# Retention plus feed-forward: groups of two units taken from two batches, and weight DMAs issued closer behind each other

## The chip, the cores and the metric

One core of one Trainium2 chip. The metric is the device time of one execution in microseconds (us); lower is better. Every comparison below uses fast executions of both kernels, taken in turn on the same chip; the experiments were run on three chips, and the kernel before took 292.2 to 292.5 us (medians) on each. A ratio is the mean time of one kernel's fast runs over that of the other's in the same rounds, so it is not quite the ratio of the medians that are quoted.

The engines are TensorE (PE in the profile; PEld is its weight load), VectorE (DVE), ScalarE (ACT), GpSimd (POOL) and SyncE (SP, which here only issues DMAs).

## The reference, cut to what matters

```
scores = 1/8 * q @ k^T                          # (8, 8, 576, 64): batch, head, position, dim
ret    = scores * gamma_h ** (i - j) * (i >= j)   # decay per head, causal
x      = (ret @ v), heads side by side            # 4608 tokens x 512
out    = relu(x @ w_in) ** 2 @ w_out              # 512 -> 2048 -> 512
```

The kernel never makes the 576 x 576 matrix. It goes along a batch in units of 128 positions with a running state R (the decayed sum of k^T v), and feeds each group of two units through the feed-forward. A batch has four full units and a tail of 64 positions; two batches share one tail unit.

## The kernel before

Eighteen groups of two units. Before, the two units of a group follow each other in one batch, so the second needs the state that the first leaves.

```
for bp in range(B // 2):
    for b in (2 * bp, 2 * bp + 1):
        units += [("full", b, c) for c in range(4)]
    units.append(("tail", 2 * bp, 4))
```

The first eight units are loaded as *pairs*: one transfer brings 256 positions of one tensor as 128 partitions, two positions to a partition, in pieces of 512 bytes. k and q of such a pair are cast and transposed on TensorE. The order of all loads at the start is fixed.

```
def add_load_pair(name, u):
    ...
        t = nc.sync.dma_start(out=x, in_=(k, q, v)[n][b, :, c * P:(c + 2) * P, :].rearrange("h (p e) d -> p h (e d)", e=2))
FIRST = ["k0", "q0", "v0", "k2", "q2", "v2", "w0", ..., "w7", "k4", "q4", "v4", "k6", "q6", "v6"]
```

The weights come as eight quarters, w0 to w3 of w_in and w4 to w7 of w_out, issued by GpSimd; the transfer casts them to fp16 on the way. Between these issues GpSimd does other work, ordered by a key (the lowest ready task first).

```
    tile_of["w", i] = nc.gpsimd.dma_start(out=dst, in_=src)
issue = add("POOL", -70 + i, 1.0, fn, deps=issues[-1:], lag=1.6 if issues else 0.0)
```

A part of that other work is the causal mask of the first two groups: half of it is copied out of PSUM by ScalarE and masked by GpSimd (`fp`), the rest is masked by VectorE (`fm`).

```
SHARED = (0, 1)
...
    if a and g in SHARED:
        c = add("ACT", -60 + e, 0.66, fc, deps=[t])
        ms.append(add("POOL", -60 + e, 0.75, fp, deps=[c]))
    else:
        ms.append(add("DVE", base + 5 + e, 0.66, fm, deps=[t] + ms))
```

## Time and profile before

| | before |
|---|---|
| time, median of 3 | 291.88 us |
| span of the profiled run | 290.6 us |
| TensorE busy | 281.6 us (97%) |
| first feed-forward matmul | 17.88 us |
| matmuls of the last w_in quarter (w3) begin | 26.77 us |
| 129th feed-forward matmul (the first of the third group) begins | 54.04 us |
| last matmul begins | 286.72 us |

The feed-forward matmuls (`ph` in the profile) always come in the same number and nearly the same order, so the time at which the n-th of them begins is a clock of the kernel's progress: a difference between two kernels at n is what one has lost by then.

### The profile page before, as it was taken

To read this page: it belongs to the slowest core of one execution; us is meant where nothing else is said; L and a number is where in the kernel's file an instruction comes from. 1 tells how busy PE (TensorE), PEld (TensorE's weight loads), DVE (VectorE), ACT (ScalarE), POOL (GpSimd) and SP (SyncE) were. 2 spreads that over 40 slices of the span, in tenths; PEclk is the share of its full clock that TensorE was granted. 3 is DMA by queue.
4 is the path that set the end of the run, shared out by engine and by line. 5 is a ranking of instruction groups with operands and counts; after the bars stand their busy time and mean duration, and the time that the engine had idled before them with its cause. 6 is when DMAs were issued, how large, how long until landed. Compare 5 with 4: busy or idle time off the path is not lost.

```text
span 290.6 us, 10028 instructions
## 1 busy us (share of the span) xinstructions
PE 281.6 (97%) x4316; PEld 233.6 (80%) x4316; DVE 197.9 (68%) x427; ACT 183.0 (63%) x351; POOL 91.4 (31%) x125
## 2 busy tenths in 40 slices
PE   8978999999999999999999999999999999999995
PEld 3557755688888888888888888888888888888884
DVE  3895369949384849675968767867767876565632
ACT  5654466486767575867767566666767676747830
POOL 5782035525433334241604251615051500000000
PEclk9999999999999999999999999999999999999999
DMA  7999999999999999997959999969699820201004
GB/s 200 275 192 181 182 300 280 215 204 193 235 173 220 208 167 235 219 214 182 190 135 210 200 192 213 204 170 187 161 182 212 167 74 2 74 2 73 2 0 147
DMA packets 139421, 49.94 MB, mean 172 GB/s; under 512 B 118128, under 2 KB 135024, under 8 KB 139376
## 3 DMA queue, kind: packets, MB, share of 16 engines
q1 hardware_dynamic: 134848, 44.84, 75.1%
q0 software_dynamic: 4224, 4.19, 9.1%
q8 instruction: 34, 0.56, 0.8%
q10 hardware_dynamic: 304, 0.26, 0.3%
q14 instruction: 11, 0.09, 0.1%
HBM read 36.70 MB, written 9.44 MB: 159 GB/s over the span
## 4 chain that ended last, share of the span: by engine, by line
PE 88%; DVE 6%; DMA 3%; ACT 1%; issue 1%; POOL 0%; DVEq 0%
PE ph L841 41%; PE po L933 34%; PE psO L339 4%; PE po L881 3%; DMA w_in<-in_moe_w_in_dram 3%; DVE rx L459 2%; PE warm L248 2%; PE psS L339 2%; PE psc L339 2%; DVE vx L396 2%; DVE R L500 1%; PE psT L417 1%; DVE xT L552 0%; ACT rl L849 0%; POOL rx L466 0%
## 5 line engine op out<-in xcount | busy, mean ns | idle before, releaser
L841 PE MATMUL ph<-xT,w_in 128*128 128x256 f16 x1152 | 140.1, 273 | 1.1 <-DMA w_in<-in_moe_w_in_dram 1.1
L841 PEld LDWEIGHTS <-w_in 128*128 128x128 f16 x1152 | 110.6, 98 | 16.6 <-DMA w_in<-in_moe_w_in_dram 1.9
L849 ACT ACTIVATE rl<-ph 128x512 f16<-128x512 f32 x144 | 84.9, 590 | 57.2 <-PE ph L841 55.8
L859 ACT ACTIVATE gT<-rl 128x512 f16<-128x512 f16 x104 | 65.6, 631 | 3.0
L933 PEld LDWEIGHTS <-gS 128*128 128x128 f16 x512 | 49.5, 98 | 6.1 <-DVE gS L910 0.2
L933 PE MATMUL po<-wT,gS 128*128 128x256 f16 x384 | 52.1, 273 | 0.0
L910 DVE TENSOR_TENSOR gS<-gT,gS 128x512 f16<-128x512 f16 x64 | 32.6, 515 | 13.4 <-ACT gT L859 12.7
L933 PEld LDWEIGHTS <-gT 128*128 128x128 f16 x384 | 37.3, 98 | 4.4
L910 DVE TENSOR_TENSOR gS<-gT 128x512 f16<-128x512 f16 x64 | 33.5, 524 | 10.7 <-ACT gT L859 10.5
L933 PE MATMUL po<-w_out,gT 128*128 128x256 f16 x256 | 34.7, 273 | 0.0
L363 POOL TENSOR_TENSOR v<-v,vdec_full 128x512 f16<-128x512 f32 x24 | 26.4, 1100 | 21.7 <-DMA v<-in_v_dram 12.2
L351 POOL CAST kq<-k 128x512 f16<-128x512 f32 x28 | 19.5, 696 | 42.3 <-DMA k<-in_k_dram 40.6
L351 POOL CAST kq<-q 128x512 f16<-128x512 f32 x28 | 19.1, 682 | 42.3 <-DMA q<-in_q_dram 42.3
L861 DVE TENSOR_TENSOR gT<-rl 128x512 f16<-128x512 f16 x40 | 19.5, 489 | 17.6 <-ACT rl L849 17.2
L956 DVE TENSOR_TENSOR o<-po,u 128x256 f32<-128x256 f32 x31 | 13.0, 420 | 14.8 <-PE po L933 9.6
L719 DVE TENSOR_TENSOR xT<-psO,gam_full 128x512 f16<-128x512 f32 x28 | 18.1, 684 | 6.8 <-PE psO L339 6.8
L946 ACT COPY u<-po 128x256 f32<-128x256 f32 x32 | 11.8, 368 | 17.2 <-PE po L933 17.0
L658 DVE TENSOR_TENSOR rT<-psc,mask 128x512 f16<-128x512 f32 x28 | 18.3, 682 | 3.9 <-PE psc L339 3.9
L933 PE MATMUL po<-w_out,gS 128*128 128x256 f16 x128 | 16.9, 273 | 0.0
L933 PE MATMUL po<-wT,gT 128*128 128x256 f16 x128 | 16.6, 273 | 0.0
L881 PE MATMUL po<-w_out,gT 128*128 128x512 f16 x64 | 15.8, 380 | 0.0
L956 DVE TENSOR_TENSOR o<-po,p 128x256 f32<-128x256 f32 x17 | 7.2, 423 | 12.5 <-ACT u L946 6.5
(81 smaller groups left out, 239.6 us busy)
## 6 DMA issues: line engine op xcount, KB each, us to landing
out_dram<-o SPq DMA_DIRECT2D x31, 256.0 KB, 3.5
k<-in_k_dram SPq DMA_DIRECT2D x24, 256.0 KB, 4.4
q<-in_q_dram SPq DMA_DIRECT2D x24, 256.0 KB, 5.0
v<-in_v_dram SPq DMA_DIRECT2D x24, 256.0 KB, 4.9
pair<-in_k_dram SPq DMA_DIRECT2D x4, 512.0 KB, 5.9
pair<-in_q_dram SPq DMA_DIRECT2D x4, 512.0 KB, 6.0
pair<-in_v_dram SPq DMA_DIRECT2D x4, 512.0 KB, 7.0
w_in<-in_moe_w_in_dram POOLq DMA_DIRECT2D x4, 512.0 KB, 7.7
```

Of the source, the lines that this page charges most:

```text
L339: nc.tensor.matmul(out_, lhsT=lhsT, rhs=rhs, start=start, stop=True, skip_group_check=True, tile_position=(64 * row, 64 * col))
L351: op(out=out_.rearrange("p (n b a d) -> p n b a d", n=2, b=2, a=2), in_=in_.rearrange("p (n a b) d -> p n b a d", n=2, a=2))
L363: nc.gpsimd.tensor_tensor(out=t, in0=tile_of["v32", u], in1=vdec[kind].rearrange("p (h o) -> p h o", o=1).to_broadcast([P, H, D]), op=ALU. ...
L658: nc.vector.tensor_tensor(out=r, in0=tile_of["psc", g][:, :, cols(s)].rearrange("p a (n i) -> p a n i", i=64), in1=mask.rearrange("p (o r ...
L841: nc.tensor.matmul(tile_of["ph", g, fb][:, j, :], lhsT=w_in16[:, m, fi * P:(fi + 1) * P], rhs=tile_of["x", g][:, m, :], start=(m == 0), st ...
L849: nc.scalar.activation(out=t, in_=tile_of["ph", g, fb], func=ACTF.Relu)
L859: nc.scalar.activation(out=t, in_=rl, func=ACTF.Square)
L861: nc.vector.tensor_tensor(out=t, in0=rl, in1=rl, op=ALU.mult)
L881: nc.tensor.matmul(tile_of["po", u], lhsT=tile_of["g", g][:, fi, s * P:(s + 1) * P], rhs=w_out16[:, fi, :], start=(fi == 0), stop=(fi == N ...
L910: nc.vector.tensor_tensor(out=Sx(k, h), in0=in0(h), in1=in1(h), op=op)
L933: nc.tensor.matmul(tile_of["pb", g, bank], lhsT=left(i), rhs=right[:, i, :], start=(start and i == 0), stop=(i == HF - 1), skip_group_chec ...
L956: nc.vector.tensor_tensor(out=o_tile(u)[:, half * HM:(half + 1) * HM], in0=bank(x), in1=tile_of[name, g], op=ALU.add)
```

## The change

The intent: with units of two batches in a group, neither needs the other's state, so a state update handles both at once (512 columns in one VectorE instruction where there were two of 256), and the first group needs no state at all. All masks go to VectorE, the squares of the first two groups to ScalarE, and GpSimd issues the weights closer together. Since the units of a pair now lie in different batches, each paired load becomes two transfers of 64 partitions. The diff, cut to its core (the renaming of states from units to groups is left out):

```diff
-        for b in (2 * bp, 2 * bp + 1):
-            units += [("full", b, c) for c in range(4)]
-        units.append(("tail", 2 * bp, 4))
+        units += [("full", b, c) for c in range(4) for b in (2 * bp, 2 * bp + 1)]
+        if bp % 2:
+            units += [("tail", b, 4) for b in (2 * bp - 2, 2 * bp)]
...
-    WARM = 28
+    WARM = 34
-    LAG = {"w0": 1.2, "k4": 0.7, "q4": 0.5}
+    LAG = {"k4": 0.7, "q4": 0.5}
-    SHARED = (0, 1)
+    SHARED = ()
...
-            t = nc.sync.dma_start(out=x, in_=(k, q, v)[n][b, :, c * P:(c + 2) * P, :].rearrange("h (p e) d -> p h (e d)", e=2))
-            if (name, u) == ("k", 4):
-                (wait for w6)
+            for s in range(2):
+                b, c = units[u + s][1:]
+                t = nc.sync.dma_start(out=x[64 * s:64 * s + 64],
+                                      in_=(k, q, v)[n][b, :, c * P:(c + 1) * P, :].rearrange("h (p e) d -> p h (e d)", e=2))
+                if (name, u, s) == ("k", 4, 0):
+                    behind(t, tile_of["w", 5])
...
+            if i == 0:
+                for s in range(2):
+                    behind(tile_of["w", i], tile_of["load", "v", 0, s])
-        issue = add("POOL", -70 + i, 1.0, fn, deps=issues[-1:], lag=1.6 if issues else 0.0)
+        issue = add("POOL", -90 + i, 0.9, fn, deps=issues[-1:] or [loaded["v", 0]], lag=1.0 if issues else 0.0)
...
+        def fr1():
+            r = tile_of["tmp", g] = work.tile([P, 2, NP * D], FP32, name="stmp", tag="stmp", bufs=1)
+            nc.vector.tensor_tensor(out=flat(r), in0=tile_of["psS", g][:, 1], in1=flat(tile_of["Rm", g]), op=ALU.add)
...
-            on_act = g >= STRASSEN and fb in (SQ_ACT if g < last_g - 1 else SQ_LATE)
+            on_act = fb in (SQ_ACT if g < last_g - 1 else SQ_LATE)
```

More of the change, by code (lines that the diff above doesn't have):

```diff
@@ L137 @@
         groups.append(list(range(first, first + n)))
-    groups[-1].reverse()
     STRASSEN = 2
@@ L148 @@
     x_pool = ctx.enter_context(tc.tile_pool(name="x", bufs=3))
-    st_pool = ctx.enter_context(tc.tile_pool(name="st", bufs=6))
+    st_pool = ctx.enter_context(tc.tile_pool(name="st", bufs=1))
     g_pool = ctx.enter_context(tc.tile_pool(name="g", bufs=3))
@@ L230 @@
     JOIN = 7
-    LAG = {"w0": 1.2, "k4": 0.7, "q4": 0.5}
+    LAG = {"k4": 0.7, "q4": 0.5}
     LAG_T, LAG_O = 1.5, 5.0
     PAIRED = 8
-    SHARED = (0, 1)
+    SHARED = ()
     FIRST = ["k0", "q0", "v0", "k2", "q2", "v2", "w0", "w1", "w2", "w3", "w4", "w5", "w6", "w7", "k4", "q4", "v4", "k6", "q6", "v6"]
     sched = Schedule(dict(ff=4, prS=1, prO=1, g=3, ld=5, wst=4, kq=7, v16=7, rT=4, x=3, rl=3, o=4, p1=2, u2=2, u4=2,
-                          R=6, Rm=6, kqT=6))
+                          R=4, Rm=2, kqT=6))
     add = sched.add
@@ L275, with behind @@
     wcast = {}
+    def behind(x, y):
+        tc.add_manual_dep(x.ins, y.ins.name, mybir.DependencyInfo(mybir.DependencyClass.Sync, mybir.DependencyReason.DATA),
+                          reason="order of transfers")
     def add_load(u):
@@ L291, in add_load_pair @@
     def add_load_pair(name, u):
-        b, c = units[u][1:]
         n = "kqv".index(name)
@@ L298, in fn @@
             x = tile_of[name + "32", u] = tile_of["stage", u][:, n % 2]
-            t = nc.sync.dma_start(out=x, in_=(k, q, v)[n][b, :, c * P:(c + 2) * P, :].rearrange("h (p e) d -> p h (e d)", e=2))
-            if (name, u) == ("k", 4):
-                tc.add_manual_dep(t.ins, tile_of["w", 6].ins.name,
-                                  mybir.DependencyInfo(mybir.DependencyClass.Sync, mybir.DependencyReason.DATA),
-                                  reason="the weights come first")
+            for s in range(2):
[4 more added lines that the diff above has]
+                    behind(t, tile_of["w", 5])
+                tile_of["load", name, u, s] = t
         loaded[name, u] = loaded[name, u + 1] = dma_task(0, 1.81 if loaded else 2.9, fn, acq=("wst",) if name != "q" else (),
@@ L315, in fn @@
             tile_of["w", i] = nc.gpsimd.dma_start(out=dst, in_=src)
-        issue = add("POOL", -70 + i, 1.0, fn, deps=issues[-1:], lag=1.6 if issues else 0.0)
-        if not issues:
-            gate.setdefault(("vx", 0), []).append(issue)
+            if i == 0:
+                for s in range(2):
+                    behind(tile_of["w", i], tile_of["load", "v", 0, s])
+        issue = add("POOL", -90 + i, 0.9, fn, deps=issues[-1:] or [loaded["v", 0]], lag=1.0 if issues else 0.0)
         issues.append(issue)
@@ L333 @@
     T = {}
+    first_waits = []
     def quad(out_, lhsT, rhs, row, col, start=True):
-        nc.tensor.matmul(out_, lhsT=lhsT, rhs=rhs, start=start, stop=True, skip_group_check=True,
-                         tile_position=(64 * row, 64 * col))
+        t = nc.tensor.matmul(out_, lhsT=lhsT, rhs=rhs, start=start, stop=True, skip_group_check=True,
+                             tile_position=(64 * row, 64 * col))
+        if first_waits:
+            behind(t, first_waits.pop())
     def half(x):
@@ L408, in add_unit_pair @@
         sched.free("wst", xs["v"])
-        for w in gate.get(("vx", u), []):
-            sched.need(w, xs["v"][0])
         T["kqT", u], T["kqT", u + 1] = [], []
@@ L435, in add_unit_pair, with decay, flat @@
         T["kvx", u] = xs["k"] + xs["v"]
+    def decay(out_, in_, n=2):
+        shape = "p (s n d) -> p s n d"
+        nc.vector.tensor_tensor(
+            out=out_.rearrange(shape, s=n, n=NP), in0=in_.rearrange(shape, s=n, n=NP),
+            in1=dec128.rearrange("p (s n o) -> p s n o", s=1, o=1).to_broadcast([P, n, NP, D]), op=ALU.mult)
+    def flat(x):
+        return x.rearrange("p s n -> p (s n)")
     def add_ret_pair(g):
@@ L488, in add_ret_pair @@
         sched.free("kq", [t])
-        chain = []
-        for s in range(2):
-            src = None if s == 0 and not carry else u + s - 1
-            def fr1(s=s, src=src):
-                r = tile_of["tmp", u + s] = work.tile([P, NP * D], FP32, name="stmp", tag="stmp", bufs=1)
-                nc.vector.tensor_tensor(out=r, in0=rT["sum"][s][:, 0:256], in1=tile_of["R", src], op=ALU.add)
-            def fr2(s=s, src=src):
-                r = tile_of["R", u + s] = st_pool.tile([P, NP * D], FP16, name="R", tag="R")
-                x = rT["sum"][s][:, 0:256] if src is None else tile_of["tmp", u + s]
-                nc.vector.tensor_tensor(
-                    out=r.rearrange("p (n d) -> p n d", d=D), in0=x.rearrange("p (n d) -> p n d", d=D),
-                    in1=dec128.rearrange("p (n o) -> p n o", o=1).to_broadcast([P, NP, D]), op=ALU.mult)
-            if src is not None:
-                chain.append(add("DVE", base + 5.5 + s, 0.42, fr1, deps=[t] + chain[-1:] + [T["R", src]]))
-                T["Rread", src].append(chain[-1])
-                sched.free("ff", chain[-1:])
-            chain.append(add("DVE", base + (6.5 if u == 0 else 5.6) + s, 0.5, fr2, deps=[t] + chain[-1:], acq=("R",)))
-            if src is None:
-                sched.free("ff", chain[-1:])
-            T["R", u + s], T["Rread", u + s] = chain[-1], []
@@ new lines, in fr1, with f, fr2 @@
+        def fr1(s):
+            def f():
+                if s == 0:
+                    tile_of["tmp", g] = work.tile([P, 2, NP * D], FP32, name="stmp", tag="stmp", bufs=1)
+                nc.vector.tensor_tensor(out=tile_of["tmp", g][:, s], in0=rT["sum"][s][:, 0:256], in1=tile_of["R", g - 1][:, s],
+                                        op=ALU.add)
+            return f
+        def fr2(s=None):
+            def f():
+                if s != 1:
+                    tile_of["R", g] = st_pool.tile([P, 2, NP * D], FP16, name="R", tag="R", bufs=4)
+                if s is None:
+                    decay(flat(tile_of["R", g]), flat(tile_of["tmp", g]))
+                else:
+                    decay(tile_of["R", g][:, s], rT["sum"][s][:, 0:256], 1)
+            return f
@@ new lines, in add_ret_pair @@
+        if carry:
+            ts = [add("DVE", base + 5.5 + s / 10, 0.42, fr1(s), deps=[t, T["R", g - 1]]) for s in range(2)]
+            sched.need(ts[1], ts[0])
+            for r in ts:
+                sched.free("ff", [r])
+            T["Rread", g - 1] += ts
+            T["R", g] = add("DVE", base + 5.7, 0.6, fr2(), deps=ts, acq=("R",))
+        else:
+            ts = []
+            for s in range(2):
+                ts.append(add("DVE", base + 26.1 + s / 10, 0.42, fr2(s), deps=[t] + ts,
+                              acq=() if s else ("R",)))
+                sched.free("ff", ts[-1:])
+            T["R", g] = ts[-1]
@@ L512, in inter @@
+        T["Rread", g] = []
         def inter(other):
@@ L515, in inter @@
                     s = a ^ other
-                    if s or carry:
-                        x = 2 * n + b
-                        put2(s, 4 * n + 2 * a + b, tile_of["R", u + s - 1][half(a), half(x)], kqT(s)[half(a), NP + x, :], a)
+                    x = 2 * n + b
+                    put2(s, 4 * n + 2 * a + b, tile_of["R", g - 1][half(a), s, half(x)], kqT(s)[half(a), NP + x, :], a)
         def put2(s, h, lhsT, rhs, row):
@@ L540, in add_ret_pair @@
         t = add("PE", base + 23.9, 0.6, fo1, deps=masked + T["kvx", u], acq=("prO",))
-        t = add("PE", base + 24, 0.75, fo2, deps=[t, T["R", u]] + ([T["R", u - 1]] if carry else []))
+        if carry:
+            t = add("PE", base + 24, 0.75, fo2, deps=[t, T["R", g - 1]])
+            T["Rread", g - 1].append(t)
         for s in range(2):
@@ L544, in add_ret_pair @@
             sched.free("kq", [t])
-            if s or carry:
-                T["Rread", u + s - 1].append(t)
         sched.free("kq", [t])
@@ L569, in cols @@
         return slice(256 * s, 256 * (s + 1))
+    place_of = {units[u]: (group_of[u], u - groups[group_of[u]][0]) for u in range(NU)}
     def states(u):
@@ L574, in states @@
         if kind == "tail":
-            return {0: ("R", u - 5), 1: ("R", u - 1)}
-        return {1: ("Rm", u), 0: ("R", u - 1)} if c else {1: ("Rm", u)}
+            return {i: ("R",) + place_of["full", b + i, 3] for i in range(2)}
+        g, s = place_of[units[u]]
+        return {1: ("Rm", g, s), 0: ("R", g - 1, s)} if c else {1: ("Rm", g, s)}
     def emit_scores(g):
@@ L620, in inter @@
                     x = 2 * n + b
-                    put(g, u, c, 4 * n + 2 * a + b, tile_of[st[c]][half(a), half(x)],
+                    put(g, u, c, 4 * n + 2 * a + b, tile_of[st[c][:2]][half(a), st[c][2], half(x)],
                         tile_of["kqT", u][half(a), NP + x, half(c)], a)
@@ L651, in out1_deps @@
     def out1_deps(g):
-        return [T[x] for u in units_of(g) for x in states(u).values()]
+        return [T[x[:2]] for u in units_of(g) for x in states(u).values()]
     def after_scores(g, t, key):
@@ L657, in fm @@
                 r = tile_of["rT", u] = work.tile([P, 2, NP, 64], FP16, name="rT", tag="rT")
-                nc.vector.tensor_tensor(
+                tile_of["masking", g] = nc.vector.tensor_tensor(
                     out=r, in0=tile_of["psc", g][:, :, cols(s)].rearrange("p a (n i) -> p a n i", i=64),
@@ L665, in after_sums @@
     def after_sums(g, t, key, res):
-        chain = []
-        for s, u in enumerate(units_of(g)):
-            if u not in full_of(g):
-                continue
-            c0 = units[u][2] == 0
-            def fr0(s=s, u=u, c0=c0):
-                r = tile_of["Rm", u] = st_pool.tile([P, NP * D], FP16, name="Rm", tag="Rm")
-                x = tile_of["psS", g][:, 0, cols(s)]
-                if c0:
-                    nc.vector.tensor_copy(out=r, in_=x)
-                else:
-                    nc.vector.tensor_tensor(out=r, in0=x, in1=tile_of["R", u - 1], op=ALU.add)
-            def fr1(s=s, u=u):
-                r = tile_of["tmp", u] = work.tile([P, NP * D], FP32, name="stmp", tag="stmp", bufs=1)
-                nc.vector.tensor_tensor(out=r, in0=tile_of["psS", g][:, 1, cols(s)], in1=tile_of["Rm", u], op=ALU.add)
-            def fr2(s=s, u=u):
-                r = tile_of["R", u] = st_pool.tile([P, NP * D], FP16, name="R", tag="R")
-                nc.vector.tensor_tensor(
-                    out=r.rearrange("p (n d) -> p n d", d=D), in0=tile_of["tmp", u].rearrange("p (n d) -> p n d", d=D),
-                    in1=dec128.rearrange("p (n o) -> p n o", o=1).to_broadcast([P, NP, D]), op=ALU.mult)
-            r0 = add("DVE", key + 0.1 + s, 0.42, fr0, deps=[t] + chain[-1:] + ([] if c0 else [T["R", u - 1]]),
-                     acq=("Rm",))
-            if not c0:
-                T["Rread", u - 1].append(r0)
-            r1 = add("DVE", key + 0.2 + s, 0.42, fr1, deps=[r0])
-            r2 = add("DVE", key + 0.3 + s, 0.5, fr2, deps=[r1], acq=("R",))
-            chain += [r0, r1, r2]
-            T["Rm", u], T["R", u], T["Rread", u], T["Rmread", u] = r0, r2, [], r1
@@ L698, in after_sums, with fr0 @@
-        if chain:
-            sched.free(res, [chain[-2]])
+        if not full_of(g):
+            return
+        c0 = units[full_of(g)[0]][2] == 0
+        def fr0():
+            r = tile_of["Rm", g] = st_pool.tile([P, 2, NP * D], FP16, name="Rm", tag="Rm", bufs=2)
+            x = tile_of["psS", g][:, 0]
+            if c0:
+                nc.vector.tensor_copy(out=flat(r), in_=x)
+            else:
+                nc.vector.tensor_tensor(out=flat(r), in0=x, in1=flat(tile_of["R", g - 1]), op=ALU.add)
@@ new lines, in fr1, with fr2 @@
+        def fr1():
+            r = tile_of["tmp", g] = work.tile([P, 2, NP * D], FP32, name="stmp", tag="stmp", bufs=1)
+            nc.vector.tensor_tensor(out=flat(r), in0=tile_of["psS", g][:, 1], in1=flat(tile_of["Rm", g]), op=ALU.add)
+        def fr2():
+            r = tile_of["R", g] = st_pool.tile([P, 2, NP * D], FP16, name="R", tag="R", bufs=4)
+            decay(flat(r), flat(tile_of["tmp", g]))
+        r0 = add("DVE", key + 0.1, 0.69, fr0, deps=[t] + ([] if c0 else [T["R", g - 1]]), acq=("Rm",))
@@ L701, in after_outs @@
+        if not c0:
+            T["Rread", g - 1].append(r0)
+        r1 = add("DVE", key + 0.2, 0.69, fr1, deps=[r0])
+        r2 = add("DVE", key + 0.3, 0.65, fr2, deps=[r1], acq=("R",))
+        T["Rm", g], T["R", g], T["Rread", g], T["Rmread", g] = r0, r2, [], r1
+        sched.free(res, [r1])
     def after_outs(g, t1, t2, key):
@@ L707, in after_outs @@
             sched.free("rT", [t2])
-            for name, ru in states(u).values():
+            for name, rg, at in states(u).values():
                 if name == "R":
-                    T["Rread", ru].append(t2)
-                else:
-                    sched.free("Rm", [t2, T["Rmread", u]])
+                    T["Rread", rg].append(t2)
+                elif at == 0:
+                    sched.free("Rm", [t2, T["Rmread", rg]])
         for u in us:
@@ L762, in f2 @@
                 emit_sums(g + 1, "prS")
+                if not full_of(g + 1):
+                    first_waits.append(tile_of["masking", g + 1])
                 emit_out2(g)
@@ L767, in add_ret @@
             t2 = add("PE", base + 30, 0.2 + QUAD * (24 * n + 16 * len(full_of(g + 1))), f2,
-                     deps=[t1] + T["masked", g] + T["masked", g + 1] + sums_deps(g + 1), acq=("prS",))
+                     deps=[t1] + T["masked", g] + T["masked", g + 1] + sums_deps(g + 1), acq=("prS",) if full_of(g + 1) else ())
             for u in units_of(g + 1):
@@ L1036 @@
             sched.free("kq", [T["kqread", u]])
-    for u in range(NU):
-        if ("Rread", u) in T:
-            sched.free("R", T["Rread", u])
+    for g in range(len(groups)):
+        if ("Rread", g) in T:
+            sched.free("R", T["Rread", g])
     for g in range(len(groups)):
```

## The prediction

> **What bounds the kernel now.** I read the page's first two parts, then the busy time in five stretches that I chose along the chain of waits, then the TensorE, GpSimd and VectorE rows of the first 60 us, and last the groups by shape.
>
> ```profile
> PE 281.6 (97%) x4316; PEld 233.6 (80%) x4316; DVE 197.9 (68%) x427; ACT 183.0 (63%) x351; POOL 91.4 (31%) x125
> ...
> DMA  7999999999999999997959999969699820201004
> ```
>
> TensorE is the bound, and DMA is full over the first half, as long as weights and inputs both have to come in. The stretches tell where time is not yet matmul:
>
> ```profile
> 0.00:17.88 17.88, 14.81 (x229) 8.03 (x229) 12.03 (x47) 10.13 (x22) 11.48 (x29) 1.00 1.03 227
> 17.88:26.77 8.89, 7.73 (x113) 5.89 (x105) 6.85 (x13) 4.60 (x8) 5.80 (x7) 1.00 1.19 184
> 26.77:57.20 30.43, 29.75 (x400) 19.42 (x400) 21.55 (x37) 16.06 (x30) 9.56 (x12) 1.00 1.11 241
> 57.20:287.00 229.80, 229.34 (x3592) 200.25 (x3584) 157.08 (x330) 152.25 (x293) 64.59 (x79) 1.00 0.80 159
> ```
>
> The columns are the stretch, its length, then busy us of PE, PEld, DVE, ACT, POOL, the clock, DMA share and GB/s. From 57.2 us to 287 us TensorE idles 0.46 us of 229.8: nothing done to VectorE there can pay. The first useful feed-forward matmul starts at 17.88 us, and most of the "busy" before it is warm-up on junk. Until 26.77 us the feed-forward waits for w_in:
>
> ```profile
> 17.88 1.92 PE L841 MATMUL ph<-xT,w_in 128*128 128x256 f16 x16
> 20.14 1.05 PE L841 MATMUL ph<-xT,w_in 128*128 128x256 f16 x8 [0.34 <-DMA w_in<-in_moe_w_in_dram]
> ...
> 23.51 2.79 PE L841 MATMUL ph<-xT,w_in 128*128 128x256 f16 x24 [0.26 <-DMA w_in<-in_moe_w_in_dram]
> 26.77 2.79 PE L841 MATMUL ph<-xT,w_in 128*128 128x256 f16 x24 [0.47 <-DMA w_in<-in_moe_w_in_dram]
> ```
>
> Each bracket is a weight quarter landing: w1 at 20.1, w2 at 23.5, w3 at 26.7. After w3 TensorE is full. So the head's bound is the time at which w3 lands, and the end comes later or earlier with it. Why the quarters are 3.3 us apart is seen on GpSimd, which issues them between its own work:
>
> ```profile
> 9.77 0.99 POOL L315 DMA_DIRECT2D w_in<-in_moe_w_in_dram  x1
> ...
> 11.34 2.29 POOL L466 TENSOR_TENSOR rx<-rx,mask 128x512 f16<-128x512 f16 x2
> 13.57 1.00 POOL L315 DMA_DIRECT2D w_in<-in_moe_w_in_dram  x1
> ...
> 15.59 0.80 POOL L315 DMA_DIRECT2D w_in<-in_moe_w_in_dram  x1
> 17.62 1.15 POOL L466 TENSOR_TENSOR rx<-rx,mask 128x512 f16<-128x512 f16 x1 [1.24 <-ACT rx L463]
> 18.73 0.81 POOL L315 DMA_DIRECT2D w_in<-in_moe_w_in_dram  x1
> ```
>
> w3 is issued only at 18.73, behind a masking step, and lands 7.99 us later (a row of the chain of waits). The four w_out parts, issued back to back from 20.67 us, come 2.5 us apart: that is the rate DMA can give.
>
> [...] the same decay multiply takes 0.41 us from PSUM, and 1.39 us from SBUF while GpSimd masks from 11.34 to 13.63:
>
> ```profile
> 11.56 0.41 DVE L500 TENSOR_TENSOR R<-psS,dec 128x256 f16<-128x256 f32 x1
> ...
> 12.54 1.39 DVE L500 TENSOR_TENSOR R<-stmp,dec 128x256 f16<-128x256 f32 x1
> ```
>
> [...] Before, only the tails are loaded as halves, in 256-byte pieces:
>
> ```profile
> 4.50:12.50 8.00, 7.58 (x102) 4.27 (x101) 5.25 (x11) 3.80 (x8) 4.00 (x7) 1.00 1.20 291
> 34.50:36.50 2.00, 2.00 (x17) 1.41 (x16) 0.85 (x2) 0.64 (x2) 0.00 (x0) 1.00 0.55 113
> 48.00:49.50 1.50, 1.50 (x38) 0.84 (x39) 1.50 (x4) 1.48 (x4) 0.61 (x1) 1.00 1.34 217
> 66.00:68.00 2.00, 2.00 (x20) 1.63 (x19) 2.00 (x3) 1.92 (x5) 1.50 (x3) 1.00 1.33 222
> ```
>
> Half tiles (48 us) and whole tiles (66 us) both give about 220 GB/s at 256 bytes, so the trace doesn't decide it. The paired loads (4.5 us) run at 291 with 512-byte pieces on whole tiles. The change cuts just these in halves.
>
> **The change part by part.**
>
> *State updates for both units at once.* Per group 2 x (0.416 + 0.423 + 0.523) = 2.72 us of VectorE become three 512-column instructions. PSUM readers of that shape take 0.68 us (the 128x512 mask rows), so about 0.68 + 0.68 + 0.65 = 2.0 us: 0.7 us less in each of 12 groups, some 8 us of VectorE. TensorE idles 0.46 us in that whole stretch, so on the path: at most 0.2 us. The number of quadrant matmuls is equal: the inter-batch terms left out of groups 0 and 2 (8 each) are now all 16 left out of group 0. The order of TensorE's work after group 4 is the same but for a few rows.
>
> *The first pair.* Group 0 no longer waits for a state: its update moves behind, and its output drops the second step. All four masks now run on VectorE: 4 x 0.64 = 2.6 us against 1.3 us before, but 4 GpSimd masks of 1.17 us, 4 ScalarE copies and the blocking that they cause go. VectorE: scaled v ends about 10.4, masks to 12.9, two decays to 13.7, q cast to 14.1, xT to 15.5 against 17.48 before. TensorE still has the second pair's sums and scores ahead of the first feed-forward matmul, and they need the second v scaled after xT, so it starts about 17.3 (estimate) against 17.88. Six more warm-up matmuls fill idle time.
>
> *Weights.* w0 waits for v's landing (VectorE scales v at 9.14) and is issued about 8.7 instead of 9.77; w1 follows one scaling, w2 one cast, w3 the second scaling; no masks between. If DMA never runs dry, w1 to w3 come at 2.55 us each: from the measured 3 gaps (20.1, 23.5, 26.7, after w0 at some 17.2) 9.5 us shrink to 7.65, so w3 lands about 24.9. TensorE then gets there itself at 24.9 to 25.5 (17.3, 56 matmuls x 0.109 = 6.1, two output steps 1.1, a mask wait). I take 25.3: **-1.5 us**.
>
> *Second batch of pairs.* Its first load now waits for w5, not w6. At 34.5 to 36.5 us DMA gave only 113 GB/s: most of this hole closes, and the loads come some 3 us earlier. What TensorE lost to them between 43 and 57 us is about 0.5 us for the second v of group 3, 0.3 for masks and some more on crossings; of 1.2 us I count **-0.8 us**.
>
> *Squares of groups 0 and 1 to ScalarE.* 14 x 0.49 us leave VectorE; ScalarE then needs some 1.08 us for relu and square of a block that TensorE makes in 0.87 us, but 64 w_out matmuls of 0.216 us are mixed in: about even, **0**.
>
> *The end.* Both last units are tails, so the last store is two half-tile DMAs on one queue where it was one. Two such took 1.54 us at 284.81 where one takes 0.34: **+0.5 us**.
>
> Sum: -1.5 - 0.8 + 0.5 = -1.8 us, 290.1 us if the split loads run as fast as before.
>
> **The rivals.** [...] v lands 1.8 us later, w0 and everything behind it too, and the second batch ends 2 to 3 us later. [...] Against: engines that also carry weight packets may hide it, and the schedule's load durations were left as they were. It would make 294.5 us. *w0 takes turns with the second pair's loads*, so v of pair 2 lands 1 to 5 us later and TensorE, in order, stands at its sums: the wait for w3 becomes a wait for v. Alone 291.5 us, with the first rival 296. *Already hidden*: TensorE reaches w3's matmuls no earlier since the masks of group 1, now all on VectorE, hold its output step: 291.5 us.
>
> **Range and chances.** [...] as the constants look tuned on the chip, I stay a little below it: 291.0 us. The range 288.3 to 296.0 covers the good case with 1.8 us to spare, and both rivals together. Faster than 286.0 would need 4 us more than what TensorE idles after 17.88 us minus fixed crossings: 0.05. Slower than 297.7 needs both rivals and more: 0.06. Within: 0.89.
>
> **What would show it.** Right: the first feed-forward matmul at 17 to 17.8 us, w3's matmuls at about 25.3 us, no DMA hole before the third k load, TensorE idle under 0.5 us from 57 us on, the last store half a microsecond later after the last matmul. Wrong: DMA at 200 to 220 GB/s instead of 291 before 10 us[...], a wait of TensorE for the second v scaling over 1 us (taking turns), relu rows queueing on ScalarE with TensorE behind them at 25 to 38 us.

## More of the kernel before

The prediction shows the rows that carry the reading. One more view is needed later, of what TensorE waits for over the whole run (in total, times, longest us):

```profile
PE ph L841 <- DMA w_in<-in_moe_w_in_dram: 1.1, 3, 0.5
PE psS L339 <- DVE vx L396: 1.0, 3, 0.3
```

Those are waits for weights and for a scaled v. No wait for a cast of k or q is among the longer ones.

## The result, and the profile after

The changed kernel took 295.77 us (median of 4, 294.41 to 295.89) where the kernel before took 292.35 in the same rounds: ratio 1.0105, 95% interval 1.0065 to 1.0144. It is 3.4 us slower, inside the predicted range of 288.3 to 296.0 us, but 0.2 us from its upper end, and on the other side of "before" from the 290.1 us that the sum of the parts gave and the 291.0 us that was forecast.

First the page of the kernel after:

```profile
PE 281.0 (96%) x4322; PEld 233.3 (79%) x4322; DVE 179.3 (61%) x378; ACT 188.1 (64%) x361; POOL 85.9 (29%) x121
...
DMA  7999999999999898999959599969997930201004
```

VectorE does 18.6 us less, TensorE as much as before, in a longer span. The chain that ended last tells where TensorE was not the bound, by engine, first before, then after:

```profile
PE 88%; DVE 6%; DMA 3%; ACT 1%; issue 1%; POOL 0%; DVEq 0%
```

```profile
PE 81%; DMA 9%; SPq 6%; POOL 2%; issue 1%; DVE 0%; POOLq 0%; DVEq 0%
```

VectorE left the chain as intended; DMA and its issuing (SPq) took 12 points more. The stretches of the prediction, after:

```profile
0.00:17.88 17.88, 12.57 (x160) 6.39 (x161) 9.27 (x45) 7.69 (x18) 7.74 (x25) 1.00 1.02 192
17.88:26.77 8.89, 7.10 (x153) 5.27 (x152) 4.94 (x9) 5.45 (x10) 5.28 (x6) 1.00 1.24 207
...
57.20:287.00 229.80, 229.31 (x3625) 200.17 (x3623) 147.90 (x296) 154.17 (x296) 65.87 (x82) 1.00 0.78 160
```

The last stretch is as before: TensorE idles 0.49 us of 229.8. All of the loss is in the first 57 us, and there in the first column of GB/s: 192 where it was 227. The short DMA windows say it more sharply:

```profile
4.50:12.50 8.00, 5.14 (x61) 2.41 (x60) 3.67 (x9) 1.96 (x4) 1.24 (x3) 1.00 1.19 220
34.50:36.50 2.00, 2.00 (x17) 1.40 (x16) 0.45 (x1) 1.76 (x4) 0.00 (x0) 1.00 1.25 208
```

From 4.5 to 12.5 us only the paired loads run, at 220 GB/s where they ran at 291, with the DMA engines busy all the same (share 1.19, before 1.20). The hole at 34.5 us is closed, as predicted. The rows of TensorE and of GpSimd:

```profile
20.85 1.92 PE L864 MATMUL ph<-xT,w_in 128*128 128x256 f16 x16
23.29 1.92 PE L864 MATMUL ph<-xT,w_in 128*128 128x256 f16 x16 [0.52 <-DMA w_in<-in_moe_w_in_dram]
...
26.23 3.99 PE L864 MATMUL ph<-xT,w_in 128*128 128x256 f16 x35
```

```profile
11.55 0.99 POOL L319 DMA_DIRECT2D w_in<-in_moe_w_in_dram  x1 [6.69 <-DMA pair<-in_v_dram]
...
19.69 0.80 POOL L319 DMA_DIRECT2D w_in<-in_moe_w_in_dram  x1
20.49 2.98 POOL L319 DMA_DIRECT2D w_out<-in_moe_w_out_dram  x4
```

GpSimd waits 6.69 us for v's landing, and w0 goes out at 11.55 us, not at 9.77. After that the quarters do come closer: they land at 20.71, 23.24, 25.79 and 28.37 us, 2.55 us apart, where before they landed 2.9 to 3.4 us apart from 17.23 on. So the part of the change that was to gain does gain, from a start that is 3.5 us later. TensorE's waits after:

```profile
PE psS L346 <- POOL vx L405: 3.2, 3, 1.3
PE psT L424 <- DVE qx L409: 1.4, 1, 1.4
...
PE ph L864 <- DMA w_in<-in_moe_w_in_dram: 0.5, 1, 0.5
```

The wait for weights fell from 1.1 to 0.5 us; in its place TensorE waits for casts of k and q and for a scaled v. Most of these wait for loads themselves: VectorE's scaling of the second v at 18.14 us, for one, was released by the landing of v. GpSimd's half of the first v also stands behind w0's issue (it begins at 12.61 us, when the issue of 11.55 us is done).

The ledger, in us of the profiled runs, by the clock of feed-forward matmuls:

| | before | after | difference |
|---|---|---|---|
| first v landed | 8.62 | 10.92 | +2.30 |
| w3's matmuls begin | 26.77 | 28.86 | +2.09 |
| 129th feed-forward matmul begins | 54.04 | 57.29 | +3.25 |
| last matmul begins | 286.72 | 289.64 | +2.92 |
| span | 290.60 | 293.92 | +3.32 |

So +2.1 in the head, +1.2 in the second batch of pairs, -0.3 in the steady state and +0.4 behind the last matmul.

### The profile page after: what moved, and what is told of

Same layout as the page of the kernel before. It is cut to its first block, busy times and chain, and to the rows that moved or that the text cites. A ratio compares the mean times of both kernels' runs of the same rounds, so it can differ in the third digit from the quotient of the medians.

```text
span 293.9 us, 10010 instructions
## 1 busy us (share of the span) xinstructions
PE 281.0 (96%) x4322; PEld 233.3 (79%) x4322; DVE 179.3 (61%) x378; ACT 188.1 (64%) x361; POOL 85.9 (29%) x121
## 4 chain that ended last, share of the span: by engine, by line
PE 81%; DMA 9%; SPq 6%; POOL 2%; issue 1%; DVE 0%; POOLq 0%; DVEq 0%
PE ph L864 39%; PE po L956 33%; SPq L303 6%; DMA w_out<-in_moe_w_out_dram 4%; PE psO L346 4%; DMA pair<-in_v_dram 2%; DMA pair<-in_q_dram 2%; PE psc L346 2%; PE psS L346 2%; PE po L904 1%; POOL qx L409 1%; POOL vx L405 1%; DVE o L979 0%; POOL w_in L319 0%; POOL w_out L319 0%
## 5 line engine op out<-in xcount | busy, mean ns | idle before, releaser
L882 ACT ACTIVATE gT<-rl 128x512 f16<-128x512 f16 x118 | 74.5, 631 | 3.4
L956 PE MATMUL po<-wT,gS 128*128 128x256 f16 x384 | 52.1, 273 | 0.0
L933 DVE TENSOR_TENSOR gS<-gT 128x512 f16<-128x512 f16 x64 | 31.7, 497 | 12.7 <-ACT gT L882 12.6
L933 DVE TENSOR_TENSOR gS<-gT,gS 128x512 f16<-128x512 f16 x64 | 29.9, 471 | 14.1 <-ACT gT L882 13.5
L360 POOL CAST kq<-k 128x512 f16<-128x512 f32 x28 | 18.9, 675 | 62.1 <-DMA k<-in_k_dram 61.7
L372 POOL TENSOR_TENSOR v<-v,vdec_full 128x512 f16<-128x512 f32 x24 | 25.9, 1077 | 18.7 <-DMA v<-in_v_dram 18.0
L360 POOL CAST kq<-q 128x512 f16<-128x512 f32 x28 | 18.4, 657 | 28.9 <-DMA q<-in_q_dram 28.8
L884 DVE TENSOR_TENSOR gT<-rl 128x512 f16<-128x512 f16 x26 | 13.3, 513 | 13.3 <-ACT rl L872 12.8
L686 DVE TENSOR_TENSOR rT<-psc,mask 128x512 f16<-128x512 f32 x28 | 18.3, 683 | 4.8 <-PE psc L346 4.7
L979 DVE TENSOR_TENSOR o<-po,p 128x256 f32<-128x256 f32 x17 | 7.2, 424 | 18.6 <-ACT u L969 9.1
L904 PE MATMUL po<-w_out,gT 128*128 128x512 f16 x64 | 15.8, 380 | 0.0
```

The source lines that it names most:

```text
L360: op(out=out_.rearrange("p (n b a d) -> p n b a d", n=2, b=2, a=2), in_=in_.rearrange("p (n a b) d -> p n b a d", n=2, a=2))
L372: nc.gpsimd.tensor_tensor(out=t, in0=tile_of["v32", u], in1=vdec[kind].rearrange("p (h o) -> p h o", o=1).to_broadcast([P, H, D]), op=ALU. ...
L686: tile_of["masking", g] = nc.vector.tensor_tensor(out=r, in0=tile_of["psc", g][:, :, cols(s)].rearrange("p a (n i) -> p a n i", i=64), in1 ...
L882: nc.scalar.activation(out=t, in_=rl, func=ACTF.Square)
L904: nc.tensor.matmul(tile_of["po", u], lhsT=tile_of["g", g][:, fi, s * P:(s + 1) * P], rhs=w_out16[:, fi, :], start=(fi == 0), stop=(fi == N ...
L933: nc.vector.tensor_tensor(out=Sx(k, h), in0=in0(h), in1=in1(h), op=op)
```

## The experiments

The main theory: a transfer into 64 neighbouring partitions is slow, whatever else is the same, and the rest of the change gains. The rivals: two transfers cost more than one through some fixed time each; 64 partitions in a transfer are slow wherever they lie; or the new order of the weights is itself the loss. One table of the measured numbers, then each run (GB/s is that of 4.5 to 12.5 us; before and after are the first pair of runs):

| run | GB/s | w3's matmuls | 129th ff | ratio to before | 95% interval |
|---|---|---|---|---|---|
| before | 291 | 26.77 | 54.04 | 1 | |
| after | 220 | 28.86 | 57.29 | 1.0105 | 1.0065 to 1.0144 |
| after, whole loads | 291 | 25.45 | 52.19 | 0.9958 | 0.9940 to 0.9977 |
| before, split loads | 226 | 29.78 | 60.54 | 1.0168 | 1.0146 to 1.0191 |
| before, closer weights | 290 | 30.16 | 58.08 | 1.0110 | 1.0070 to 1.0149 |
| after, two queues | 224 | 28.59 | 56.86 | 1.0107 | 1.0082 to 1.0131 |
| all but the two batches | 291 | 25.49 | 52.21 | 0.9945 | 0.9930 to 0.9959 |
| before, split by heads | 289 | 26.92 | 56.47 | 1.0043 | 1.0018 to 1.0068 |
| before, odd and even | 288 | 27.60 | 55.37 | 1.0066 | 1.0044 to 1.0088 |
| before, weights and masks | 291 | 25.49 | 52.21 | 0.9937 | 0.9914 to 0.9961 |
| before, companions | 291 | 25.64 | 52.36 | 0.9942 | 0.9917 to 0.9968 |
| before, masks alone | 291 | 25.51 | 52.33 | 0.9962 | 0.9930 to 0.9995 |

The instants come from one profiled execution each, the ratios from all. In three of these executions the granted clock fell to 0.50 for 3.41 us: "before, split loads" and "before, closer weights" from 18.7 us on, "before, odd and even" from 18.3 us on. Their two instants contain that dip (by an estimate, 3.41 us at 0.50, worth at most 1.7 us of TensorE), their GB/s do not. The profiled execution of "before, split loads" was also the slowest of its five (299.25 us; the median is 297.19).

### The kernel after with whole loads

Its output is wrong on purpose (relative error 0.635): each paired load takes 256 positions of one batch again, in one transfer, while the program goes on as if they were of two batches. The work is the same.

```diff
-            for s in range(2):
-                t = nc.sync.dma_start(out=x[64 * s:64 * s + 64], in_=... (unit u + s))
+            t = nc.sync.dma_start(out=x, in_=... (both of one batch))
```

> The changed kernel, but each paired load is again one transfer of 128 partitions (from one batch, so the result is wrong on purpose; bytes and order stay). Theory (half-tile loads are slower, 222 instead of 291 GB/s before 12 us): DMA is back at about 290 GB/s there, v has landed by about 8.7 us instead of 10.9, w3's matmuls start at about 25.3 to 26 us instead of 28.9, and the time falls by 3 to 5 us to 291 to 292.5. Rival (the four masks on VectorE, the later state and the squares on ScalarE hold the head): DMA is faster but the first feed-forward matmul and w3's stay within 1 us of where they are, and the time stays above 294.5.

Measured: 290.96 us, 4.8 us less than the kernel after. Window and TensorE rows:

```profile
4.50:12.50 8.00, 6.99 (x99) 3.42 (x98) 5.45 (x13) 2.82 (x6) 3.80 (x7) 1.00 1.20 291
```

```profile
17.74 1.92 PE L861 MATMUL ph<-xT,w_in 128*128 128x256 f16 x16
...
22.82 5.41 PE L861 MATMUL ph<-xT,w_in 128*128 128x256 f16 x48
```

The rate is back at 291, and at 22.82 us 48 matmuls begin, those of w2 and w3 among them, without a bracket: TensorE no longer waits for these quarters. w3's matmuls begin at 25.45 us; the prediction had 25.3. With the split undone, the change gains some 1.2 us of the 1.8 that the sum of its parts had promised. So the split loads are the loss.

### The kernel before with split loads

The reverse: the kernel before, its paired loads cut into the lower and the upper 64 partitions, nothing else. The result stays correct.

> The kernel before with nothing changed but each paired load cut into two transfers of 64 partitions (right result). Theory (half-tile loads): 220 to 230 GB/s before 12 us instead of 291, w3's matmuls 2.5 to 3.5 us later than 26.8, and 3 to 5 us more than before. Rival (something else in the change): within 1 us of before.

Measured: 297.19 us, ratio 1.0168, 5.0 us more than before, with this window:

```profile
4.50:12.50 8.00, 5.30 (x91) 2.58 (x89) 3.77 (x9) 3.04 (x6) 2.22 (x4) 1.00 1.22 226
```

The cost of the split is the same from both sides: 4.8 us taken away from the kernel after, 5.0 us added to the kernel before.

### What of the split costs: two cuts of another shape

Both keep two transfers of 262 kB in 512-byte pieces; only what a transfer covers differs. One cuts by heads (128 partitions, four heads), the other takes every second partition (64 partitions, spread over all).

```diff
+ heads:     out=x[:, 4 * s:4 * s + 4],  in_=...[b, 4 * s:4 * s + 4, ...]
+ odd, even: out=x[s:s + 127:2],         in_=..."h (p s e) d -> s p h (e d)"[s]
```

> The kernel before, each paired load cut into two transfers of 128 partitions and four heads each: the same number of transfers, the same 262 KB and the same 512-byte pieces as in the run that cut them by 64 partitions, so only the partitions differ; a correct result. Theory (a transfer into 64 neighbouring partitions is what is slow): 280 to 295 GB/s at 4.5 to 12.5 us and time within 0.4% of before. Rival (a fixed cost per transfer of about 0.5 us: 1.17 us for 262 KB and 1.81 for 524 KB make 0.53 us fixed): 220 to 228 GB/s, w3's matmuls near 29.8 and time 1.5 to 1.9% above before.

> The kernel before, each paired load cut into two transfers of 64 partitions each, but the even and the odd partitions instead of the lower and the upper 64; a correct result. [...] Theory[...]: 270 to 295 GB/s at 4.5 to 12.5 us and time within 0.5% of before. Rival (64 partitions in one transfer are slow wherever they lie, or two transfers are slower than one): 220 to 228 GB/s and time 1.5 to 1.9% above before. [...]

Measured, first by heads, then odd and even:

```profile
4.50:12.50 8.00, 6.81 (x96) 3.46 (x95) 4.68 (x10) 3.55 (x7) 3.31 (x6) 1.00 1.13 289
```

```profile
4.50:12.50 8.00, 6.21 (x96) 3.07 (x95) 4.63 (x10) 3.55 (x7) 3.18 (x6) 1.00 1.10 288
```

Both rates are those of whole loads. Neither the number of transfers, nor their size, nor 64 partitions as such make 226 GB/s: it takes 64 *neighbouring* partitions. What makes neighbouring partitions slower, these runs do not show.

The time tells a second thing: I expected "within 0.4%" and "within 0.5%", and these runs are 0.43% and 0.66% slower, some 1.3 and 1.9 us. That is at the edge of what was expected (both intervals hold the expected bound), but both intervals lie above 1. So twice as many transfers, which is what the two runs share (twelve loads cut in two, six in each batch of pairs), have a cost of their own at full rate. If the lower-and-upper cut paid it as well, its 5.0 us would be some 1.3 to 1.9 us of it and 3.0 to 3.7 us of the lower rate (1.0168 less 1.0066, or less 1.0043, of 292.2 us). That subtraction is an estimate and not shown. The trace has a part of the cost at 4.5 to 6.0 us: there DMA moved 255 and 233 GB/s at a share of 0.87 and 0.82, where the kernel before moved 295 at 1.19, so its engines lacked work. The lower-and-upper cut shows no such gap (221 GB/s at 1.19), so the lower rate may account for more than 3.7 us. The rest I have not taken apart; in both runs the first v is complete 0.7 to 0.8 us later than before (9.33 and 9.45 us), and w0 goes out that much later (10.48 and 10.59 us).

### The kernel after, with two queues

If halves are served one after the other, two queues might serve a lower and an upper half at once. The upper halves of the first three loads are issued from ScalarE's queue at the start:

> The changed kernel with the upper halves of the first three paired loads issued on ScalarE's queue at the very start, so that lower and upper halves are in flight together (right result). Theory[...]: both together come in at about 290 GB/s, v has landed by about 9 us instead of 10.9, w3's matmuls start 1.5 to 2 us earlier, and the time falls by about 1.5 us. Rival (each transfer costs by its count or its issue, not by where it writes): v lands no earlier than 10.5 us and the time stays within 0.7 us of the changed kernel.

Measured: 295.43 us, no better than the kernel after, as the rival had it. v's lower half landed at 10.36 us, far from the theory's 9. The window:

```profile
4.50:12.50 8.00, 6.20 (x62) 2.75 (x61) 4.22 (x10) 3.53 (x12) 1.72 (x4) 1.00 1.22 224
```

In the trace's packets the two queues alternate by whole transfers: from 3.75 to 4.25 us nearly all bytes come from SyncE's queue, from 4.75 to 5.5 us from ScalarE's, then the other again, and so on to 8.5 us. So the halves never ran beside each other for long, and this run could not show what they would do if they did.

### The kernel before with the closer weights alone

The weight issues and the gate of the second batch as in the kernel after, with everything else as before, GpSimd's masks too.

> The kernel before with the other part alone: weights issued from v's landing on, ahead of GpSimd's masks and closer behind each other, first load of the second batch behind w5. Theory (the weights' gaps were worth 1.5 us and the hole before the second batch 0.8, as predicted): w1 to w3 come 2.55 us apart, w3's matmuls at about 25 to 25.5 us, and the time is 1.5 to 2.5 us under before. Rival (TensorE gets no earlier to w3 since its own chain over masks and states holds it): less than 0.7 us gained.

Measured: 296.09 us, ratio 1.0110. This missed every theory that I had: I expected a gain or nothing. The weights did come early (w3 landed at 25.30 us), yet its matmuls began at 30.16 us. GpSimd's rows, and two of TensorE's, show where the time went in the profiled execution:

```profile
8.97 0.99 POOL L318 DMA_DIRECT2D w_in<-in_moe_w_in_dram  x1 [4.12 <-ACT kqT L431]
...
11.86 2.28 POOL L469 TENSOR_TENSOR rx<-rx,mask 128x512 f16<-128x512 f16 x2
14.09 0.80 POOL L318 DMA_DIRECT2D w_in<-in_moe_w_in_dram  x1
14.90 0.62 POOL L403 CAST kx<-pair 128x512 f16<-128x512 f32 x1
...
24.02 2.54 POOL L469 TENSOR_TENSOR rx<-rx,mask 128x512 f16<-128x512 f16 x2 [5.06 <-ACT rx L466]
```

```profile
18.67 3.56 PE L844 MATMUL ph<-xT,w_in 128*128 128x256 f16 x16 [0.94 <-ACT kqT L431]
22.15 0.64 PE L342 MATMUL psc<-kqT 64*64 64x128 f16 x32
```

The masks of the first group stand at 11.86 to 14.14 us behind two weight issues, only some 0.5 us later than before (11.34 to 13.63). What moved more is the work behind them: GpSimd's cast of the second pair's k runs at 14.90 us instead of 10.76, and the second group's scores (`psc`) begin at 22.15 us, behind the first 16 feed-forward matmuls, instead of at 16.49. In this program ScalarE copies these scores and GpSimd masks the copies, so GpSimd sits idle for 5.06 us, and the masks of the second group come at 24.02 us; in the kernel before they began at 17.62 and 19.56 us. TensorE waits 2.2 us in all for GpSimd's masks ("psO <- POOL rx", three times, the longest 1.0 us). There is a second loss in this profile, and it is a surprise:

```profile
18.00:20.00 2.00, 1.33 (x7) 1.00 (x8) 1.83 (x5) 1.02 (x3) 0.96 (x2) 0.68 1.25 207
20.00:22.00 2.00, 2.00 (x11) 1.25 (x9) 0.69 (x2) 0.60 (x1) 0.00 (x0) 0.50 1.24 205
```

The granted clock (third column from the end) falls to 0.68 and 0.50 at 18 to 22 us, behind a stretch with stalls (TensorE was busy 1.02 us of 14 to 16 and 1.50 us of 16 to 18; in the kernel before, which kept its clock, 1.56 and 1.11 us); from these two windows I estimate its cost at 2 x 0.32 + 2 x 0.50, at most some 1.6 us of TensorE at full clock. Of the six executions the two with a mean clock of 1.000 and 0.998 took 293.06 and 293.68 us, the four with 0.994 took 296.04 to 296.97. So without the dip this kernel is still about 1 us slower than before, and with it 4. The dip goes with the longer times here; that the stalls cause it was not tested. In "before, odd and even" the execution with the dip was the fastest of four (293.30 us), so a dip does not always cost time.

### Masks, companions, and the version that beats both

Four runs take the head's changes apart, all on the kernel before with whole loads of one batch, all correct. "All but the two batches" has the closer weights, all masks on VectorE, the squares of groups 0 and 1 on ScalarE and 34 warm-up matmuls. "Weights and masks" has the first two of these. "Companions" has all but the closer weights. "Masks alone" is one word:

```diff
-    SHARED = (0, 1)
+    SHARED = ()
```

> The kernel before with the weight part of the change (DMAs closer behind each other, gated by the load of v), its companions (all masks on VectorE, squares of the first two groups on ScalarE, 34 warm-up matmuls), but with whole 128-partition loads and the pairs of one batch: everything of the change's head except the two-batch loads; a correct result. My theory (the weights gain 1.3 us at the head if the loads run at 290 GB/s and no mask stands behind a weight issue): w3's matmuls at 25.4 to 26.0 instead of 26.77, the 128th ff matmul at or below 54.0, time 0.3 to 0.6% below before (290.5 to 291.5 when before is 292.2). Rival (the masks on GpSimd were not what made the weights-only run slow; the closer weight DMAs themselves hurt): w3's matmuls near 30 and time 1% above before. Second rival (the gain of the whole-load run came from joint states and two-batch pairs, not from the weights): time equal to before.

> The kernel before with the closer weight DMAs and all masks on VectorE, and nothing else of the change (squares of the first two groups stay on VectorE, 28 warm-up matmuls, whole loads, pairs of one batch); a correct result. It differs from the weights-only run in one word: where the masks of the first two groups run. Theory (GpSimd's masks behind the weight issues were what made the weights-only run slow): w3's matmuls at 25.4 to 26.2, not 30.2, and time 0.2 to 0.6% below before. Rival (the squares moved to ScalarE were needed too, because VectorE then has masks and squares at once): w3's matmuls after 27 and time at or above before.

> The kernel before with all masks on VectorE, squares of the first two groups on ScalarE and 34 warm-up matmuls, but with the weight DMAs as before; a correct result. Theory (the gain of the whole-load run with closer weights is the weights'): w3's matmuls stay at 26.5 to 27.0 and time within 0.2% of before. Rival (the companions made the gain, the spacing of the weights is hidden): time 0.4 to 0.6% below before and w3's matmuls below 26.

> The kernel before with one word changed: the masks of the first two groups run on VectorE instead of GpSimd. Weight DMAs, squares, warm-up, loads and pairs as before; a correct result. Theory (it is GpSimd's masks that stand between the weight issues and hold them apart, and moving them is the whole gain): weights' issues 4 to 7 closer together than 1 us, weights landing 2.5 to 2.6 us apart, w3's matmuls at 25.4 to 26.0 and time 0.4 to 0.8% below before, as in the run with all three companions. Rival (the squares on ScalarE or the longer warm-up have a share in it): w3's matmuls at 26 to 26.8 and time 0 to 0.3% below before.

Measured: 290.76, 290.90, 290.97 and 291.13 us; the four intervals overlap, so I don't rank them, and each lies below 1. All four beat the kernel before by 1.1 to 1.8 us (0.38 to 0.63%) and the kernel after by 4.6 to 5.0 us.

The first two came as expected ("weights and masks" gained 0.63% where 0.2 to 0.6 was written). "Companions" fell to its rival: without any change of the weight code the gain is whole, and w3's matmuls begin at 25.64 us, where I had expected 26.5 to 27.0. The reason is in GpSimd's rows of "masks alone":

```profile
9.54 0.99 POOL L315 DMA_DIRECT2D w_in<-in_moe_w_in_dram  x1
...
15.05 1.55 POOL L315 DMA_DIRECT2D w_in<-in_moe_w_in_dram  x2
16.58 2.98 POOL L315 DMA_DIRECT2D w_out<-in_moe_w_out_dram  x4
```

Against the prediction's rows of the kernel before: no mask stands between the issues, the fourth goes out at some 15.8 us instead of 18.73, and the quarters land 2.4 to 2.6 us apart by themselves. The wider spacing was never the weight code's; it went with the four masks. By which way they held the quarters apart is shown only in part. In the kernel before the weights' packets thin out twice: 127 began at 15.5 to 16.5 us (200 in masks alone), behind an issue of w1 that came at 13.57 us instead of 11.09, and 181 at 23.5 to 25.0 us (302), when w3 and w4 had been issued more than 2 us before. The second gap is no late issue, and what made it stays open. The masks' place is thus the one part of the whole change that gains alone, 0.38% (an interval of 0.05 to 0.70%). Closer weight code alone loses; with the masks moved it adds nothing that shows (0.9937 against 0.9962 and 0.9942, with overlapping intervals).

The comparison of "all but the two batches" (0.9945) with the kernel after on whole loads (0.9958) isolates the rest, mainly the two-batch groups and the joint states: nothing that shows in the time (overlapping intervals, on two chips), though VectorE does 9 us less (180.6 against 189.9 us busy up to 287 us).

## Why the prediction was right or wrong

**The range held; the size and the sign did not.** The sum said -1.8 us; the traces say +3.3 us. The range held because it had been widened to take in both rivals together, and one of them came alone and 1.3 us larger than written: that is more luck than foresight. (The chances written behind the range, 0.05, 0.06 and 0.89, belong to 286.0 to 297.7 us and not to 288.3 to 296.0.) The sum stands on the words "if the split loads run as fast as before". They ran at 220 GB/s instead of 291, and that is what turned the sign. The first feed-forward matmul, written at 17.3 us, came at 20.85 us with split loads and at 17.74 us with whole ones.

*Weights, -1.5 us at w3.* Failed as a sum, right in its mechanism where the loads run at full rate. Their distance went to 2.55 us as written, and with whole loads w3's matmuls begin at 25.45 us (25.3 written). In the kernel after they begin at 28.86. Two details were wrong as well: I put the gain down to closer issues and moved masks together, but moving the masks alone gains as much, as far as the intervals can tell; and w0 gains nothing from an earlier issue. With whole loads it went out at 8.93 to 9.04 us instead of 9.77, and its first packet still came at 12.9 us, as before, when the loads ahead had drained.

*Second batch of pairs, -0.8 us.* Measured +1.2 us with split loads (3.25 less 2.09) and -0.5 us with whole ones (-1.85 less -1.32). The hole at 34.5 us closed as predicted; the loads behind it were slower. v of the last pair landed at 53.0 us, some 4 us later (its last packet ended at 52.1 us, before at 47.9).

*Steady state, at most 0.2 us.* Measured 0.3 us (2.92 less 3.25), and TensorE's idle time there is 0.49 us of 229.8. A joint update takes 0.681 + 0.688 + 0.749 = 2.12 us by the group rows, where I had 2.0 from the mask rows.

*Squares, 0.* No wait of TensorE for ScalarE appears from 25 to 38 us. Right.

*The end, +0.5 us.* The time behind the last matmul grew by 0.40 us (3.88 to 4.28). But kernels with the end of before show 3.60 to 4.33 us there, so this run doesn't show that the tails did it. It stays open.

*The rivals.* The first, that half-tile loads come in slower, came true in full, and its working was close: they ran at 220 GB/s instead of 291, v landed 2.30 us later (1.8 written, the author's estimate, which no trace of the kernel before showed), and the time was 295.77 us (294.5 written). It was given a weight of 0.3, which made the mean 291.4 us. The step that failed is this weighing, with which the forecast stayed below that mean: the argument was that "the constants look tuned on the chip", which is evidence about the author and none about the loads, while the trace of the kernel before, with 217 GB/s for half tiles and 222 for whole ones, both in 256-byte pieces, left the question open. That the engines' weight packets might hide it could have been excluded from the trace of the kernel before, in which no weight packet runs before 12.9 us. "w0 takes turns with the second pair's loads" did not happen: w0's first packet came at 16.0 us, as the loads ran out (their last packet ended at 17.1 us). "Already hidden" did not happen either: with whole loads TensorE reaches w3's matmuls 1.3 us earlier.

## What to carry to other kernels

When a change of data order splits a load, ask first which partitions each piece covers: here one transfer into 64 neighbouring partitions ran at 220 to 226 GB/s where whole tiles, head halves and odd-even halves ran at 288 to 291, and the cut as a whole cost 4.8 us where the rest of the change gained 1.2. Work that shares an engine with DMA issues can hold the transfers apart (with four masks on GpSimd the weight quarters landed 2.9 to 3.4 us apart, with them on VectorE 2.4 to 2.6); look at what stands between two issues before tuning the issues themselves. And an engine with 9 us less work (VectorE, with whole loads) gave nothing that shows, since it was not what the others waited for.
